# A transformer block on one core: four re-orderings in the first 25 microseconds

## The chip, the cores and the metric

The kernel runs on one core of a Trainium2 chip. A core has five engines that run side by side and wait for one another by semaphores: TensorE (PE, matmuls; PEld is its weight load), VectorE (DVE), ScalarE (ACT), GpSimd (POOL) and SyncE (SP, which here only issues DMAs). Every engine works through its own instructions strictly in the order of the program, so an instruction that waits also holds up all those behind it on its engine. ACT can issue DMAs too. Data lie in SBUF; matmul results go to PSUM, whose banks are handed around.

The metric is the device time of one execution in microseconds; of several runs the median is taken.

## The reference

The kernel computes a layernorm, and from it, in parallel, sliding-window attention and a gated feed-forward network, and adds both to the input:

```
x  = A_x                                   # 1 x 2048 x 448, bf16
xn = (x - mean) / sqrt(var + 1e-5)
q, k, v = xn @ wqkv                        # 16 heads of 28
p  = softmax(q k^T / sqrt(28)), a query sees the 256 keys up to its own
out = x + (p v) @ wo + (gelu(xn @ w_gate) * (xn @ w_up)) @ w_down    # inner width 1792
```

## The kernel before

**Tiling.** The 2048 rows are 16 x tiles of 128 rows, and four query blocks (`qb`) of 512 rows, that is four tiles each. The feature dimension 448 is three chunks of 128 and a half chunk of 64. `xnT` holds the normalised rows transposed, with the half chunk stored twice (partitions 0 to 63 and 64 to 127), so that two half matmuls can run on the two halves of the PE array: `mm3` makes the three full chunks of a product, `mm_half` the half one. A head has 28 columns, but 32 partitions: `wqp`, `wkp` and `w3p` are copies of the q and k weights with heads spread to 32 columns ("padding copies"), made by `pads(engine, dst, groups)`; a group is four heads. `w3p` holds the half chunk of both. Later, `fill_pads` writes into the four spare columns of each head, with nine small copies and then three more and a memset.

**Order.** All instructions are put out in the order written (a manual schedule). The start of the kernel is straight code (lines 662 to 708): for tiles 0 to 3 `stat` (DVE: bn_stats, bn_aggr), `rstd` (ACT: Ln, then Exp of -0.5 times it), `norm` (DVE, and POOL for the last 64 columns of tiles 1 and 2), `transp` (PE transposes, copied from PSUM by ACT or DVE). Between them stand v's products of tiles 0 to 3 (`v_dense` the three chunks, `v_half` the half one, `v_copy` from PSUM to `v_sb`) and the q and k projections of group 0 (`proj`, `qk_halves`, `qk_copies`: q by ACT, k by DVE). `make_masks` (POOL) writes a table needed from query block 1 on.

**The attention of query block 0** has 12 steps, three for each group of four heads. A step: products held back from the step before are finished (`held` feeds: half matmuls and copies), scores (PE, into one PSUM area of four banks that is free again when the Exp of the step before is done), Exp (ACT, L604), masks by `affine_select` (POOL, L518), then filler matmuls from the feeds (projections of the next groups, `gen_up` products, block 1's projections), and at last one entry of `aux`: `ahead` in step 0 (norm of tile 4), `ahead2` in step 1, `ahead3` in step 2, `fill_pads` in steps 3 and 4. The feeds take PSUM banks in the ring m, m, d; a bank can be written again when its earlier content was copied out. In group 1, `gen_qk` gets `others`, the half products of v's tiles 2 and 3 (the "second excursion" to half matmuls); the bank of tile 3's v is the one that group 2's q takes next. Tiles 4 and up are transposed by DMA (`dma_transp`, on SP). After `ahead3`, SP issues the later weights (`loads`).

**Input DMAs** are issued by SP and ACT in the order of lines 126 to 147. Each engine has one queue, and both queues are served by the same 16 DMA engines. L130 (ACT) brings the q and k weights of heads 0 to 3, L138 (SP) those of heads 4 to 15, q's half first, then k's.

After query block 0's attention come, four times, the gated products, and then the attention of the next block mixed with the down projection. The change does not touch these.

Of the kernel before, what the change touches and what calls it, by code (L numbers as in the profile page):

```python
# [15 lines left out]
S, D, H, Dh, F = 2048, 448, 16, 28, 1792  # L16
# [59 lines left out]
def kernel(  # L76
# [11 lines left out]
    nc = tc.nc  # L88
# [18 lines left out]
    xv = A_x.rearrange("b (n p) d -> p (b n) d", p=P)  # L107
# [3 lines left out]
    x_sb = const.tile([P, NT, D], bf16, name="x_sb")  # L111
    wv = const.tile([P, 4, D], bf16, name="wv")
    v_sb = const.tile([P, NT, H, 32], bf16, name="v_sb")
    wraw = blk.tile([P, 4, 2 * D], bf16, name="wraw", tag="hT")
# [7 lines left out]
    def rows(w, c0, n):  # L122
        return w[c0 * P:(c0 + n) * P, :].rearrange("(c p) n -> p c n", p=P)

    wqk = rows(A_wqkv, 0, 3)[:, :, 0:2 * D]
    nc.sync.dma_start(out=x_sb[:, 0, :], in_=xv[:, 0, :])
    nc.scalar.dma_start(out=x_sb[:, 1, :], in_=xv[:, 1, :])
    nc.sync.dma_start(out=x_sb[:, 2:4, :], in_=xv[:, 2:4, :])
    for c in (0, D):
        nc.scalar.dma_start(out=wraw[:, 0:3, c:c + 4 * Dh], in_=wqk[:, :, c:c + 4 * Dh])  # L130
# [38 lines left out]
    wqp = const.tile([P, 3, H, 32], bf16, name="wqp")  # L169
    wkp = const.tile([P, 3, H, 32], bf16, name="wkp")  # L170
    w3p = const.tile([P, H, 32], bf16, name="w3p")
# [15 lines left out]
    def warmup(n):  # L187
        wps = phase[0].pool.tile([P, 2, QB], f32, name="wps", tag="s")
        for i in range(n):
            nc.tensor.matmul(wps[:, i % 2, :], lhsT=warm[:, 0:P], rhs=warm[:, 0:QB], start=True, stop=True)  # L190


    def stat(t):
        st = work.tile([P, nc.vector.BN_STATS_DIM], f32, name="st")
        nc.vector.bn_stats(out=st[:, :], in_=x_sb[:, t, :])  # L195
        nc.vector.bn_aggr(out=mv_all[:, t, :], in_=st[:, :])

    def rstd(t, n):
        lnv = work.tile([P, 4], f32, name="lnv")
        nc.scalar.activation(out=lnv[:, 0:n], in_=mv_all[:, t:t + n, 1], func=ACT.Ln, bias=eps_t[:, 0:1], scale=1.0)  # L200
        nc.scalar.activation(out=rstd_all[:, t:t + n], in_=lnv[:, 0:n], func=ACT.Exp, scale=-0.5)
# [3 lines left out]
    def norm(t):  # L205
        xn = work.tile([P, 4, P], bf16, name="xn", bufs=4)
        xf = xn[:, :, :].rearrange("p a b -> p (a b)")
        for eng, lo, n, src in ((nc.vector, 0, D, 0), (nc.gpsimd if t in (1, 2) else nc.vector, D, 64, 384)):
            eng.tensor_scalar(out=xf[:, lo:lo + n], in0=x_sb[:, t, src:src + n], scalar1=mv_all[:, t, 0:1],
                              scalar2=rstd_all[:, t:t + 1], op0=ALU.subtract, op1=ALU.mult)  # L210
        xns[t] = xn

    def dma_transp(t):

        nc.sync.dma_start_transpose(out=xnT[:, :, t * P:(t + 1) * P], in_=xns.pop(t)[:, :, :].rearrange("p a b -> p (a b)"))

    def transp(t, n, copy, tag):

        tp = psum.tile([P, 2, 4, P], bf16, name="tp", tag=tag, bufs=2 if tag == "m" else 1)
        for i in range(n):  # L220
            xn = xns.pop(t + i)
            for c in range(4):
                nc.tensor.transpose(out=tp[:, i, c, :], in_=xn[:, c, :], identity=ident[:, :])
        copy(out=xnT[:, :, t * P:(t + n) * P].rearrange("p c (i q) -> p i c q", q=P), in_=tp[:, 0:n, :, :])

    def mm3(ps, lhs, rhs, start, stop):
        for c in range(3):
            nc.tensor.matmul(ps, lhsT=lhs(c), rhs=rhs(c), start=start and c == 0, stop=stop and c == 2,  # L228
                             skip_group_check=True)

    def mm_half(ps, lhs, rhs, hi, start, stop):
        p0 = 64 * hi
        nc.tensor.matmul(ps, lhsT=lhs[p0:p0 + 64], rhs=rhs[p0:p0 + 64], start=start, stop=stop,  # L233
                         tile_position=(p0, 0), skip_group_check=True)
# [4 lines left out]
    def bank(name):  # L239

        tag = ring[0][ring[1] % len(ring[0])]
        ring[1] += 1
        return psum.tile([P, QB], f32, name=name, tag=tag, bufs=2 if tag == "m" else 1)


    def v_dense(t, pv):
        mm3(pv, lambda c: xnT[:, c, t * P:(t + 1) * P], lambda c: wv[:, c, :], True, False)

    def v_half(t, pv):
        mm_half(pv, xnT[:, 3, t * P:(t + 1) * P], wv[:, 3, :], t % 2, False, True)  # L250

    def v_copy(t, pv, copy):
        copy(out=v_sb[:, t, :, 0:Dh], in_=pv.rearrange("p (h d) -> p h d", d=Dh))  # L253
# [15 lines left out]
    def proj(ps, w, qb, g):  # L269
        mm3(ps, lambda c: w[:, c, 4 * g:4 * g + 4, :].rearrange("p h d -> p (h d)"), lambda c: xnT[:, c, qb * QB:(qb + 1) * QB],  # L270
            True, False)

    def qk_halves(qb, g, pq, pk):
        w3 = w3p[:, 4 * g:4 * g + 4, :].rearrange("p h d -> p (h d)")
        for hi, ps in enumerate((pq, pk)):
            mm_half(ps, w3, xnT[:, 3, qb * QB:(qb + 1) * QB], hi, False, True)

    def qk_copies(qb, g, pq, pk):
        ts = slice(qb * QB, (qb + 1) * QB)
        nc.scalar.copy(out=qT[:, g, ts], in_=pq)  # L280
        nc.vector.tensor_copy(out=kT[:, g, ts], in_=pk)
        done.add((qb, g))

    def gen_qk(qb, gs, others=()):

        for g in gs:
            pq = bank("pq")[:, :]
            proj(pq, wqp, qb, g)
            if qb and g == 3:
                yield 650  # L290
                ts = slice(qb * QB, (qb + 1) * QB)
                nc.tensor.matmul(pq, lhsT=w3p[:, 12:16, :].rearrange("p h d -> p (h d)"), rhs=xnT[:, 3, ts], start=False, stop=True,
                                 skip_group_check=True)
                nc.scalar.copy(out=qT[:, 3, ts], in_=pq)
                done.add((qb, 3))
                yield -220
                return
            yield 650
            pk = bank("pk")[:, :]
            proj(pk, wkp, qb, g)  # L300
            yield 650, HOLD
            qk_halves(qb, g, pq, pk)
            for t, pv in others:
                v_half(t, pv)
            if others:
                v_copy(*others[1], nc.vector.tensor_copy)
            qk_copies(qb, g, pq, pk)
            others = ()
            yield -360
# [36 lines left out]
    def gen_proj(qb):  # L346
        yield from gen_v(qb, (4 * qb, 4 * qb + 2))
        yield from gen_qk(qb, range(4))
# [299 lines left out]
    def pads(eng, dst, gs):  # L648

        hs = slice(4 * gs.start, 4 * gs.stop)  # L650
        c0 = D * (dst is wkp)
        src = wraw[:, 0:3, c0 + Dh * hs.start:c0 + Dh * hs.stop]
        eng(out=dst[:, :, hs, 0:Dh], in_=src.rearrange("p c (h d) -> p c h d", d=Dh))
# [13 lines left out]
    norm(0)  # L667
    transp(0, 1, nc.scalar.copy, "o")
    stat(2)
    norm(1)  # L670
    rstd(2, 1)
    warmup(1)
    transp(1, 1, nc.scalar.copy, "d")
    stat(3)
# [1 line left out]
    pvs = [bank("pv")[:, 0:D]]  # L676
    v_dense(0, pvs[0])
    norm(2)
    pads(nc.vector.tensor_copy, wqp, slice(0, 1))
    nc.vector.tensor_copy(out=w3p[:, :, 0:Dh], in_=wraw[:, 3, 0:D].rearrange("p (h d) -> p h d", d=Dh))  # L680
    pads(nc.scalar.copy, wkp, slice(0, 1))
    transp(2, 1, nc.scalar.copy, "o")
    pvs.append(bank("pv")[:, 0:D])
    v_dense(1, pvs[1])
    norm(3)
# [4 lines left out]
    pq, pk = (phase[0].pool.tile([P, 2, QB], f32, name="s0", tag="s")[:, 0, :] for _ in range(2))  # L690
    proj(pq, wqp, 0, 0)
    proj(pk, wkp, 0, 0)
    stat(4)
    stat(5)
    rstd(4, 2)
# [1 line left out]
    for t in range(2):  # L697
        v_half(t, pvs[t])
    qk_copies(0, 0, pq, pk)
    for dst in (wqp, wkp):  # L700
        pads(nc.vector.tensor_copy, dst, slice(1, 2))
    v_copy(0, pvs[0], nc.scalar.copy)
    v_copy(1, pvs[1], nc.vector.tensor_copy)
    pvs.append(alone("pv", "d"))
# [9 lines left out]
    def ahead2():  # L714
        stat(6)
        stat(7)
        rstd(6, 2)
        norm(5)
        dma_transp(5)

    def ahead3():
        for t in (6, 7):
            norm(t)
            dma_transp(t)
        v_copy(2, pvs[2], nc.vector.tensor_copy)
        loads()

    def loads():

        nc.sync.dma_start(out=x_sb[:, 12:16, :], in_=xv[:, 12:16, :])  # L730
        nc.sync.dma_start(out=wgu3[0:64, :], in_=B_w_gate[384:448, :])
        nc.sync.dma_start(out=wug3[64:128, :], in_=B_w_gate[384:448, :])
        nc.sync.dma_start(out=wg[:, :, :], in_=rows(B_w_gate, 0, 3))
        wo_v = A_wo.rearrange("(g j d) n -> j d g n", g=4, j=4)
        for j in range(4):
            nc.sync.dma_start(out=wo[32 * j:32 * j + Dh, :, :], in_=wo_v[j])
        for k in range(0, NF, 4):
            n = min(4, NF - k)
            nc.sync.dma_start(out=wd[:, k:k + n, :], in_=rows(B_w_down, k, n))
# [189 lines left out]
```

## Time and profile before

| what | value |
|---|---|
| runs, median of 3 | 223.92 us (223.68 to 224.28) |
| profiled execution: span from first to last instruction | 222.5 us |
| profiled execution: own time | not listed; the median lies 1.42 us above the span |
| PE busy | 211.6 us (95%) |
| DVE busy | 156.3 us (70%) |
| ACT busy | 132.9 us (60%) |
| POOL busy | 44.7 us (20%) |
| mean granted PE clock | 0.994 |
| chain that ended last | PE 91%, DVE 4%, issue 1%, DMA 1% |

How to read it: "busy" is the time in which an engine had an instruction running. The chain that ended last is followed back from the last instruction, at each step to what released it; its shares show where a microsecond counts. Times in rows of the timeline are start and length in us, followed by the engine, the line of the kernel, the operation, what it writes and reads, and in square brackets the idle time before it and what ended it. Rows of one kind that follow each other are merged (x2 is two of them). On DVE and ACT an instruction's row often starts some 0.09 us before the last one's ends. The profiled execution is one, the slowest core's; the runs give the times.

### The profile page before, as it was taken

Reading aid. Unit: us, or ns where it says so; the run is one execution under the profiler, and the core shown is the slowest. Engines: PE = TensorE matmul, PEld = TensorE weight load, DVE = VectorE, ACT = ScalarE, POOL = GpSimd, SP = SyncE. Lnnn points to the kernel's source line nnn. Section 1 sums busy time; section 2 is a strip of 40 time slices with the busy share of each in tenths; the row PEclk is TensorE's granted clock in tenths of the full one; section 3 lists DMA queues with packets and bytes.
Section 4 is the critical chain, followed back from the end, with each engine's and each line's share of the span. In section 5 each row is a group of like instructions: output and inputs, shape, how many; then the busy total and the mean of one; then the engine's idle time right before and its main releaser. Section 6 shows DMA issues by size and latency. Waiting matters only on the chain.

```text
span 222.5 us, 5330 instructions
## 1 busy us (share of the span) xinstructions
PE 211.6 (95%) x2215; PEld 94.5 (42%) x2240; DVE 156.3 (70%) x370; ACT 132.9 (60%) x129; POOL 44.7 (20%) x65
## 2 busy tenths in 40 slices
PE   6899999999999999999999999999999999999990
PEld 2333333344444454444444445444444435434470
DVE  5989996799666983778566895585454999479210
ACT  4597788644878874533868886323767778453000
POOL 5763687320000220022000030022000022022000
PEclk9999999999999999999999999999999999999997
DMA  6994899104100001001500001200000000000011
GB/s 190 312 327 47 195 327 289 20 2 72 45 3 21 24 24 31 16 19 28 70 0 24 24 0 45 43 0 0 0 4 24 24 0 24 21 0 4 22 45 27
DMA packets 18046, 13.31 MB, mean 60 GB/s; under 512 B 8704, under 2 KB 16992, under 8 KB 18016
## 3 DMA queue, kind: packets, MB, share of 16 engines
q1 hardware_dynamic: 17072, 12.62, 21.6%
q8 instruction: 19, 0.31, 0.6%
q10 hardware_dynamic: 944, 0.29, 0.5%
q14 instruction: 11, 0.09, 0.2%
HBM read 9.15 MB, written 2.18 MB: 51 GB/s over the span
## 4 chain that ended last, share of the span: by engine, by line
PE 91%; DVE 4%; issue 1%; DMA 1%; ACT 0%; DVEq 0%
PE po L375 20%; PE gt L228 17%; PE u L228 12%; PE sc L600 6%; PE po L370 6%; PE gt L233 5%; PE ue L228 5%; PE ov L560 5%; PE pq L228 4%; PE pv L228 4%; PE pk L228 3%; PE pq L233 2%; DVE st L195 1%; PE ue L233 1%; DMA x_sb<-in_A_x_dram 1%
## 5 line engine op out<-in xcount | busy, mean ns | idle before, releaser
L604 ACT ACTIVATE p_sb<-sc 128x2048 bf16<-128x2048 f32 (+2 forms) x42 | 73.8, 1758 | 12.6 <-PE sc L600 7.3
L375 PE MATMUL po<-wd,hT 128*128 128x448 bf16 (+1 forms) x238 | 50.0, 342 | 0.0
L452 ACT ACTIVATE ge<-gt 128x1024 bf16<-128x1024 f32 x28 | 28.7, 1024 | 33.6 <-PE u L233 20.9
L527 POOL TENSOR_TENSOR oN<-oc,l 128x512 bf16<-128x512 f32 x12 | 16.0, 1333 | 138.6 <-DVE l L544 88.2
L228 PE MATMUL gt<-xnT,wg 128*128 128x512 bf16 x161 | 38.9, 380 | 1.0 <-issue 0.9
L456 DVE TENSOR_TENSOR hT<-ge,u 128x512 bf16<-128x512 bf16 x40 | 25.6, 682 | 9.7 <-ACT ge L452 9.6
L375 PEld LDWEIGHTS <-hT 128*128 128x128 bf16 x238 | 21.4, 98 | 18.6 <-issue 2.6
L228 PE MATMUL u<-xnT,wu 128*128 128x512 bf16 x116 | 28.8, 379 | 0.2
L508 DVE TENSOR_TENSOR p_sb<-p_sb,masks 128x256 bf16<-128x256 bf16 (+1 forms) x90 | 27.2, 356 | 0.4 <-ACT p_sb L604 0.4
L228 PEld LDWEIGHTS <-wg 128*128 128x128 bf16 x168 | 15.1, 98 | 21.5 <-issue 5.2
L228 PEld LDWEIGHTS <-wu 128*128 128x128 bf16 x168 | 16.0, 98 | 19.2 <-issue 1.0
L549 DVE TENSOR_TENSOR oc<-oc,ov 128x512 f32<-128x512 f32 x12 | 8.3, 688 | 18.3 <-ACT oc L548 18.3
L600 PE MATMUL sc<-qT,kT 28*64 28x320 bf16 (+7 forms) x640 | 16.9, 263 | 0.1
L380 DVE TENSOR_TENSOR res<-po,x_sb 128x448 bf16<-128x448 f32 (+1 forms) x17 | 9.9, 585 | 8.7 <-PE po L375 8.6
L370 PE MATMUL po<-wo,oN 128*128 128x448 bf16 (+1 forms) x68 | 15.9, 343 | 0.0
L518 POOL TENSOR_SCALAR_AFFINE_SELECT p_sb<-p_sb 128x512 bf16<-128x512 bf16 (+1 forms) x20 | 14.2, 731 | 8.3 <-ACT p_sb L604 8.1
L409 DVE CAST hT<-ue 128x512 bf16<-128x512 f32 x16 | 10.2, 680 | 6.3 <-PE ue L233 6.2
L548 ACT COPY oc<-ov 128x512 f32<-128x512 f32 x12 | 7.0, 584 | 11.9 <-PE ov L560 11.9
L233 PE MATMUL gt<-xnT,wgu 64*128 64x512 bf16 x48 | 13.2, 379 | 0.0
L228 PE MATMUL pq<-xnT,wqp 128*128 128x512 bf16 x36 | 11.7, 380 | 0.7 <-DVE v_sb L253 0.3
L534 DVE STREAM_TRANSPOSE l<-oc 128x512 f32<-128x512 f32 x16 | 11.3, 704 | 1.4 <-POOL oN L527 1.2
L228 PE MATMUL ue<-xnT,wu 128*128 128x512 bf16 x43 | 11.6, 380 | 0.4 <-issue 0.2
(87 smaller groups left out, 235.4 us busy)
## 6 DMA issues: line engine op xcount, KB each, us to landing
out_dram<-res SPq DMA_DIRECT2D x15, 112.0 KB
x_sb<-in_A_x_dram SPq DMA_DIRECT2D x3, 448.0 KB
wu<-in_B_w_up_dram SPq DMA_DIRECT2D x1, 1344.0 KB
wg<-in_B_w_gate_dram SPq DMA_DIRECT2D x1, 1344.0 KB
wd<-in_B_w_down_dram SPq DMA_DIRECT2D x3, 448.0 KB
wraw<-in_A_wqkv_dram SPq DMA_DIRECT2D x2, 252.0 KB
wo<-in_A_wo_dram SPq DMA_DIRECT2D x4, 98.0 KB
wv<-in_A_wqkv_dram SPq DMA_DIRECT2D x1, 336.0 KB
```

Of the source, the lines that this page charges most:

```text
L228: nc.tensor.matmul(ps, lhsT=lhs(c), rhs=rhs(c), start=start and c == 0, stop=stop and c == 2, skip_group_check=True)
L233: nc.tensor.matmul(ps, lhsT=lhs[p0:p0 + 64], rhs=rhs[p0:p0 + 64], start=start, stop=stop, tile_position=(p0, 0), skip_group_check=True)
L370: nc.tensor.matmul(po[:, 0:w], lhsT=oN[:, g, cs], rhs=wo[:, g, lo:up], start=(g == 0), stop=False, skip_group_check=True)
L375: nc.tensor.matmul(po[:, 0:w], lhsT=hT[:, f, cs], rhs=wd[:, f, lo:up], start=False, stop=(f == NF - 1), skip_group_check=True)
L452: nc.scalar.activation(out=ge[:, :, :], in_=pr["gt"][:, :, :], func=ACT.Gelu_apprx_tanh)
L456: nc.vector.tensor_tensor(out=hT[:, f + i, :], in0=ge[:, i, :], in1=u[:, :], op=ALU.mult)
L508: nc.vector.tensor_tensor(out=reg, in0=reg, in1=m, op=ALU.mult)
L518: nc.gpsimd.affine_select(out=reg, in_=reg, pattern=mid + [[1 if diag else -1, min(w, P)]], compare_op=ALU.is_ge, fill=0.0, base=0 if diag ...
L527: nc.gpsimd.tensor_tensor(out=oN[:, g, :], in0=oc[:, :], in1=inv, op=ALU.mult)
L534: nc.vector.transpose(out=l1[:, :, :].rearrange("p a b -> p (a b)"), in_=oc[:, :])
L600: nc.tensor.matmul(ss[k0:k0 + nk, j, col:col + nq], lhsT=kT[r, g, kt * P + k0:kt * P + k0 + nk], rhs=qT[r, g, qb * QB + q0:qb * QB + q0 + ...
L604: nc.scalar.activation(out=p_sb[:, :, 0:ncol], in_=ss[:, :, 0:ncol], func=ACT.Exp, scale=SCALE)
```

## The change

The diff has five places.

1. Tile 0 of x is loaded in two halves of 64 partitions, one by SP and one by ACT. Tile 1 moves from ACT's queue to SP's, ahead of tiles 2 and 3.
2. The first padding copies (group 0): `wqp` goes from DVE to ACT, `wkp` stays on ACT, and both now stand behind `transp(2)`'s copy; `w3p`'s copy goes from DVE to POOL, behind the norms of tiles 1 and 2 and ahead of `make_masks`.
3. The second ones (group 1) go from DVE, where they stood behind group 0's k copy, to ACT, ahead of `rstd(4, 2)`.
4. In `gen_qk`, v's half products stand ahead of `qk_halves` where there are any (group 1 of block 0).
5. `rstd(6, 2)` (Ln and Exp on ACT) moves from `ahead2` (step 1) to the head of `ahead3` (step 2).

`rstd(2, 1)` is also written ahead of `norm(1)`; the two have no engine in common, so each engine's order stays the same.

```diff
-    nc.sync.dma_start(out=x_sb[:, 0, :], in_=xv[:, 0, :])
-    nc.scalar.dma_start(out=x_sb[:, 1, :], in_=xv[:, 1, :])
+    nc.sync.dma_start(out=x_sb[0:64, 0, :], in_=xv[0:64, 0, :])
+    nc.scalar.dma_start(out=x_sb[64:128, 0, :], in_=xv[64:128, 0, :])
+    nc.sync.dma_start(out=x_sb[:, 1, :], in_=xv[:, 1, :])
...
             yield 650, HOLD
-            qk_halves(qb, g, pq, pk)
             for t, pv in others:
                 v_half(t, pv)
+            qk_halves(qb, g, pq, pk)
...
     stat(2)
+    rstd(2, 1)
     norm(1)
-    rstd(2, 1)
...
     norm(2)
-    pads(nc.vector.tensor_copy, wqp, slice(0, 1))
-    nc.vector.tensor_copy(out=w3p[:, :, 0:Dh], in_=wraw[:, 3, 0:D].rearrange("p (h d) -> p h d", d=Dh))
-    pads(nc.scalar.copy, wkp, slice(0, 1))
     transp(2, 1, nc.scalar.copy, "o")
+    for dst in (wqp, wkp):
+        pads(nc.scalar.copy, dst, slice(0, 1))
+    nc.gpsimd.tensor_copy(out=w3p[:, :, 0:Dh], in_=wraw[:, 3, 0:D].rearrange("p (h d) -> p h d", d=Dh))
...
     proj(pk, wkp, 0, 0)
+    for dst in (wqp, wkp):
+        pads(nc.scalar.copy, dst, slice(1, 2))
     stat(4)
     stat(5)
     rstd(4, 2)
...
     qk_copies(0, 0, pq, pk)
-    for dst in (wqp, wkp):
-        pads(nc.vector.tensor_copy, dst, slice(1, 2))
     v_copy(0, pvs[0], nc.scalar.copy)
...
     def ahead2():
         stat(6)
         stat(7)
-        rstd(6, 2)
         norm(5)
         dma_transp(5)
...
     def ahead3():
+        rstd(6, 2)
         for t in (6, 7):
```

## The prediction

> **What bounds the kernel now.** I read four views in this order: busy time by stretch, the chain of waits in order of time, who waited for whom, and the timeline of single engines. The table by stretch comes first (columns: busy us and count of PE, PE weight loads, DVE, ACT, POOL, then clock, DMA share, GB/s).
>
> ```profile
> 14.70:20.00 5.30, 4.58 (x33) 1.69 (x34) 5.20 (x13) 4.16 (x8) 3.46 (x5) 1.00 0.56 133
> 20.00:26.00 6.00, 5.95 (x47) 2.18 (x47) 5.89 (x22) 4.52 (x4) 3.36 (x6) 1.00 0.74 103
> 26.00:36.40 10.40, 10.29 (x97) 4.00 (x98) 10.06 (x23) 9.39 (x10) 7.77 (x10) 1.00 1.07 318
> ```
>
> From 18.5 us on PE has no idle time to speak of, so a microsecond that it is early or late there is kept to the end. But DVE is just as full from 14.7 to 36.4 us: PE can only stay ahead by what DVE gains too. Everything the change touches ends before 26 us.
>
> ```profile
> 7.45 0.89 DVE wqp L653
> 8.34 0.12 DVE w3p L680
> 8.46 0.31 DVE xn L209
> ...
> 14.73 0.62 DVE v_sb L253
> ...
> 17.46 0.30 ACT lnv L200
> 17.79 0.20 ACT rstd_all L201
> 17.99 0.48 ACT qT L280
> ```
>
> These are the pieces of the chain that the edits aim at: the padding copies between two norms, v's copy, and the Ln/Exp that holds up a q copy.
>
> **The first x tile.** DVE's first statistics wait 1.25 us for x and start at 3.40, when tile 0 has landed. Tiles 0 and 1 share the DMA engines (between 2.4 and 2.8 us the two queues carry 53% and 48%); at that window's 327 GB/s, 224 KB take 0.7 us, so tile 0 alone lands up to 0.35 us earlier. I take 0.3 (0 to 0.4). Tile 1 now follows on SP at 1.26 us; with tile 0's 2.58 us from issue to landing it is there at 3.84, when the second statistics would start (4.17 - 0.33). No cost. But every later load of SP moves back by one issue of about 0.45 us (0.40 to 0.48 in the rows).
>
> **The first padding copies.** They leave DVE's order between norm(2) and norm(3), where wqp and w3p take 7.45 to 8.46.
>
> ```profile
> 7.42 0.85 POOL L155 MEMSET masks<- 128x768 bf16 x1
> 7.45 0.89 DVE L653 COPY wqp<-wraw 128x336 bf16<-128x336 bf16 x1
> 7.91 0.46 ACT L653 COPY wkp<-wraw 128x336 bf16<-128x336 bf16 x1
> 11.23 0.29 ACT L200 ACTIVATE lnv<-mv_all,eps_t 128x2 f32<-128x2 f32 x1 [2.38 <-DVE mv_all L196]
> ```
>
> The reader should see that DVE's copy takes 0.89 us here and 0.28 at 12.22: it ends 0.07 after the POOL memset at its side. This pattern returns below. norm(3) would be bound by its own Exp instead: 8.00 less 0.3, so 7.7 in place of 8.38. On POOL the w3p copy costs between 0.63 (a 512-column select) and 1.27 us (L527, two inputs); I take 0.8, from about 7.3, with the memset of masks behind it. norm(3) is a copy-like DVE op from SBUF to SBUF and can be held in the same way: its start lies between 7.7 and, behind both POOL ops, 9.4. I take 8.1, a gain of 0.3; the masks have until the Exp of step 0 (14.75) and end near 14.1. ACT's two copies (2 x 0.46 behind transp(2)'s copy at 8.0 to 8.6) end near 9.1, before PE needs wqp and wkp near 9.5 and 10.1.
>
> **The second copies, ahead of rstd(4).** ACT idles 2.38 us before 11.23, and two copies of 0.46 look free. But wkp's heads 4 to 7 come with the last of L138's loads. Up to it queue q1 carries 1.89 MB (sizes of the DMA list); it had moved 1.92 MB by 9.5 us, some of it already wu's, and the trace's completion records of that load end at 10.55, two engines late. The extra SP issue moves that to 10.7 to 11.0; I take L = 10.85. Queued behind the waiting copy on ACT: Ln 0.29 and Exp 0.20 of rstd(4), qT's copy 0.57, v_sb's copy 0.54. With the overlaps of the rows (each starts some 0.09 before the last ends) qT ends at L + 1.39 and v_sb at L + 1.83, and PE's next projection, which reuses v_sb's bank, starts at 12.71. It starts at 12.72 now. So the gain of some 0.6 us at the start is taken back by this wait: net 0 (0.3 gained if L is 10.55; 0.3 lost if it is 11.1 or norm(3) is held long). DVE loses two copies of 0.28 and 0.25 at 12.22, where it has slack until 14.73: nothing.
>
> **v's half tiles first.** Their matmuls start at 14.11 instead of 14.33, so DVE's v_sb copy and PE's pq behind it (it waits 0.26 for that copy) come 0.22 earlier; q's copy on ACT starts 14.73 instead of 14.64, hidden behind Exp 0, which ends at 14.75.
>
> **Ln/Exp a step later.**
>
> ```profile
> 15.19 1.45 ACT L604 ACTIVATE p_sb<-sc 128x1536 bf16<-128x1536 f32 x1
> 17.46 0.29 ACT L200 ACTIVATE lnv<-mv_all,eps_t 128x2 f32<-128x2 f32 x1 [0.82 <-DVE mv_all L196]
> 18.36 1.03 ACT L604 ACTIVATE p_sb<-sc 128x1024 bf16<-128x1024 f32 x1
> 19.68 0.58 ACT L280 CAST qT<-pq 128x512 bf16<-128x512 f32 x1 [0.29 <-PE pk L233]
> ```
>
> Without the 0.82 us of waiting, qT of group 2 starts at 16.97 (its matmuls end at 17.18 - 0.23), the Exp of step 2 runs 17.45 to 18.48 instead of 18.36 to 19.39, and PE's 0.36 us wait at pk goes. Behind it now stand Ln and Exp (0.42, to 18.90), then qT of group 3 (18.89, before 19.68) and the Exp of step 3, which ends at 21.26 instead of 22.04. norm(6) waits for that Exp until 18.92 and for POOL's select of step 2 (18.54 to 19.2), before 18.79. The four norms, v_copy(2) and kT follow: kT ends near 21.13, before 21.33. SP's transposes of tiles 6 and 7 and the loads behind them move by under 0.2 us; PE reads those tiles at 26.4 and wg at 39.5. So ACT and PE gain 0.78 here, DVE only 0.20.
>
> **What is late next.** DVE's nine small copies of fill_pads come right after kT.
>
> ```profile
> 20.66 0.67 DVE L281 CAST kT<-pk 128x512 bf16<-128x512 f32 x1
> 21.26 0.15 DVE L318 COPY wqp<-wraw 128x16 bf16<-128x16 bf16 x1
> ...
> 21.90 0.16 DVE L320 COPY wkp<-wraw 128x48 bf16<-128x48 bf16 x1
> 21.98 1.27 DVE L409 CAST hT<-ue 128x512 bf16<-128x512 f32 x2
> ...
> 22.11 1.68 POOL L518 TENSOR_SCALAR_AFFINE_SELECT p_sb<-p_sb 128x1024 bf16<-128x1024 bf16 x2 [1.94 <-ACT p_sb L604]
> ```
>
> They end at 22.06 and POOL's selects of step 3 start at 22.11: they just miss. Afterwards the copies run 21.06 to 21.86 and the selects start at 21.33, whatever the start of the kernel gains, since both hang on the Exp of step 2. DVE ops from SBUF to SBUF that meet a POOL op end just after it: norm(5) took 0.72 instead of 0.37 beside the select that ended at 17.93, the last norm 0.60 instead of 0.29 beside 19.46 to 20.18. No row shows small copies in that place. Their price is 0 if they slip through, 1.1 (the 128x1024 select) if they are held once, 1.7 if also by the second. A row decides for held once: 48 columns take only 10 ns longer than 16 (164 against 155), which is the fast rate of the copies that were held (116 to 130 ns for 336 columns more), not that of a cast from PSUM (680 ns for 512).
>
> [...]
>
> **Sum.** Held once, hT's copies start at 22.9 instead of 21.98, then 0.68 + 0.68 + the oc copy 0.68 + fill_pads' second part 0.5; hT of the next pair is copied by 25.80 instead of 25.02. PE's matmul pv, which started right at that copy (25.08), starts at 25.83: +0.75, with 0 from the start of the kernel. Span 222.5 + 0.75 = 223.25. The profiled execution's own time is not listed; the median 223.92 of the runs lies 1.42 above its span, and I keep that: 224.67, rounded 224.7.
>
> **Rivals.**
> 1. Held by both selects (norm(5), issued at 17.34 just as one select followed another, waited for the second): 0.6 more, 225.3.
> 2. The small copies slip through, the other side. Then PE gains only DVE's part: hT's copy at 24.80 in place of 25.02 (PE can't use its 0.76 us, its bank is freed then), -0.26: 223.65. The edits would do what they say locally and little at the end.
> 3. As 2, and the second wraw load is not later than now (L at most 10.5): another 0.4, 223.25 or less. It decides below an L of about 10.5; for it: only two of the sixteen completions came after 9.95. Against it: SP issues it all behind one more load.
> 4. L that early, but the copies are held: 224.3.
>
> **Chances.** Forecast 0.40, its own range 224.3 to 225.1; rival 1 0.20; rival 2 0.16; rival 3 0.16; rival 4 0.08. 0.3% is 0.67 us (also about what a measurement here can tell from no change): faster is below 223.25, slower above 224.59. Faster: most of rival 3 and some of 2, 0.17. Slower: all of rival 1 and three quarters of the forecast, 0.50. Same: 0.33. The range 223.1 to 225.5 takes in all cases but the ends of 1 and 3.
>
> **What would show it.** The first statistics near 3.1; norm(3) near 8.1; ACT idle until 10.7 to 11.0 before the second wkp copy and qT at 11.7; PE's pq of group 1 still near 12.7; no wait of pk on qT; the Exp of step 3 over near 21.3; the nine copies torn apart, one or more above 0.5 us beside a POOL select. If these keep 0.16 us, or if the start is 0.3 us ahead at 12.7, the forecast is wrong.

## The result, and the profile after

| | before | after |
|---|---|---|
| runs, median | 223.96 us (223.68 to 224.28, 6 runs) | 227.26 us (226.75 to 228.94, 6 runs) |
| profiled execution: span | 222.5 us | 225.2 us (own time 226.97) |
| mean granted PE clock | 0.994 (profiled execution) | 0.997 (profiled execution; 0.992 to 0.999 in the runs) |
| last residual (DVE `res`) starts | 217.34 | 219.65 |

The kernel became slower: the ratio is 1.0147, with a 95% interval of 1.0128 to 1.0167. The prediction was 224.7, with a range of 223.1 to 225.5.

The busy time by stretch, for the same three stretches as before (columns as there):

```profile
14.70:20.00 5.30, 5.14 (x35) 1.81 (x37) 4.03 (x9) 4.87 (x7) 3.26 (x5) 1.00 0.96 178
20.00:26.00 6.00, 4.67 (x46) 1.65 (x44) 5.86 (x18) 3.85 (x4) 3.26 (x5) 1.00 0.45 74
26.00:36.40 10.40, 10.08 (x84) 3.72 (x82) 9.99 (x26) 8.28 (x9) 6.19 (x8) 1.00 1.05 292
```

In the second stretch PE is busy for 4.67 us in place of 5.95, while DVE is as full as before (5.86). In the first, PE is busier than before (5.14 against 4.58), though the work in it is not quite the same, since the kernel is some 1.1 us late there: the two waits that the change aimed at, PE's 0.26 us for v's copy and 0.36 us for qT behind Ln/Exp, are gone. The loss lies on both sides of it. The chain of waits in order of time (start, length, what) names both places:

```profile
12.53 0.53 DVE v_sb L254
13.06 0.31 DVE wqp L654
...
13.39 0.40 PE sc L601 x8
...
13.83 0.81 PE pq L229 x3
...
21.79 0.60 DVE kT L282
...
22.63 1.00 DVE wqp L319
...
23.79 0.43 DVE wqp L319
...
24.38 1.19 DVE hT L410 x2
```

The first place is group 1's projection, `pq` at 13.83, which stood at 12.72 before. The timeline of ACT shows why:

```profile
9.74 0.47 ACT L654 COPY wqp<-wraw 128x336 bf16<-128x336 bf16 x1 [0.23 <-DMA wraw<-in_A_wqkv_dram]
11.97 0.47 ACT L654 COPY wkp<-wraw 128x336 bf16<-128x336 bf16 x1 [1.75 <-DMA wraw<-in_A_wqkv_dram]
...
12.78 0.57 ACT L281 CAST qT<-s 128x512 bf16<-128x512 f32 x1
13.24 0.54 ACT L254 CAST v_sb<-pv 128x448 bf16<-128x448 f32 x1
```

The second wkp copy waits 1.75 us for the last load of q and k weights, which lands at 11.94 (10.55 before). Ln, Exp, qT's copy and v's copy stand behind it on ACT. The scores need qT, which is there at 13.35, and start at 13.39; `pq` comes behind the scores and behind v's copy, which ends at 13.78. (The chain puts the scores' wait down to DVE's `wqp` copy, which runs beside them; the scores read qT and kT.)

The second place is the nine small copies. Here are DVE, POOL and PE in their timelines (one fence for each):

```profile
22.31 0.16 DVE L319 COPY wqp<-wraw 128x16 bf16<-128x16 bf16 x1
...
22.55 1.08 DVE L319 COPY wqp<-wraw 128x16 bf16<-128x16 bf16 x1
23.54 0.17 DVE L321 COPY wqp<-wraw 128x48 bf16<-128x48 bf16 x1
23.63 0.16 DVE L321 COPY wkp<-wraw 128x48 bf16<-128x48 bf16 x1
23.72 0.50 DVE L319 COPY wqp<-wraw 128x16 bf16<-128x16 bf16 x1
...
24.30 1.27 DVE L410 CAST hT<-ue 128x512 bf16<-128x512 f32 x2
```

```profile
22.49 1.71 POOL L519 TENSOR_SCALAR_AFFINE_SELECT p_sb<-p_sb 128x1024 bf16<-128x1024 bf16 x2 [2.16 <-ACT p_sb L605]
```

```profile
25.03 0.81 PE L229 MATMUL ue<-xnT,wu 128*128 128x512 bf16 x3 [1.33 <-DVE hT L410]
```

Two of the nine take 1.08 and 0.50 us in place of 0.16, each ending just behind a select. hT's copies start at 24.30 (21.98 before), and PE waits 1.33 us for them. Counted by the starts of the Exp instructions, the kernel is 1.03 us late in step 0, 1.12 in step 1, 0.23 in step 2, 0.38 in steps 3 and 4, 1.87 in step 5 and 2.30 in step 6, and stays 2.30 late to the last residual. Another 0.4 us lies between the start of the last residual and the end of the span (5.6 against 5.2 us). That stretch took 5.2 to 5.9 us in the seven profiles of kernels that split tile 0, and 4.7 to 5.4 us in the nine of kernels that do not. Whether the split causes this was not tested, and what makes the stretch vary was not looked for.

### The profile page after: what moved, and what is told of

It is laid out like the page before. It is cut to its first block, busy times and chain, and to the rows that moved or that the text cites. A ratio compares the mean times of both kernels' runs of the same rounds, so it can differ in the third digit from the quotient of the medians.

```text
span 225.2 us, 5357 instructions
## 1 busy us (share of the span) xinstructions
PE 214.1 (95%) x2240; PEld 94.8 (42%) x2240; DVE 156.6 (70%) x366; ACT 134.3 (60%) x132; POOL 44.9 (20%) x66
## 3 DMA queue, kind: packets, MB, share of 16 engines
HBM read 9.15 MB, written 2.18 MB: 50 GB/s over the span
## 4 chain that ended last, share of the span: by engine, by line
PE 89%; DVE 6%; ACT 1%; DMA 1%; issue 0%; DVEq 0%
PE po L376 20%; PE gt L229 17%; PE u L229 12%; PE po L371 6%; PE sc L601 6%; PE gt L234 5%; PE ov L561 4%; PE pq L229 4%; PE ue L229 4%; PE pv L229 3%; PE pk L229 3%; PE pq L234 1%; DMA x_sb<-in_A_x_dram 1%; DVE xn L210 1%; PE pv L234 1%; PE ue L234 1%
## 5 line engine op out<-in xcount | busy, mean ns | idle before, releaser
L229 PE MATMUL gt<-xnT,wg 128*128 128x512 bf16 x168 | 40.3, 380 | 0.0
L229 PE MATMUL ue<-xnT,wu 128*128 128x512 bf16 x48 | 12.2, 380 | 1.3 <-DVE hT L410 1.3
L254 DVE CAST v_sb<-pv 128x448 bf16<-128x448 f32 x13 | 7.7, 614 | 7.0 <-PE pv L234 7.0
L229 PE MATMUL pq<-xnT,wqp 128*128 128x512 bf16 x45 | 12.2, 380 | 0.2
```

## The experiments

The loss has two candidates, so the runs undo single parts in the changed kernel (first four), make single parts alone in the kernel before (the next), and then take the two costs by themselves. "Before" in each is the kernel before on the same chip: 224.2 us beside the first four, 224.09 beside the next three and the variant with parts 2, 4 and 5, 224.31 beside the order, split and three-warm-up kernels and part 5 with the copies out of the way, 224.28 beside the five warm-ups and the last kernel. A kernel is compared by how far its median lies above that of its own before; for the whole change that is 3.30 us. Behind it stands the ratio with its 95% interval, which is the better guide where the runs spread: part 1 alone lies 1.41 us above by medians and 1.8 by its ratio.

### Undoing one part of the change

**Second padding copies back on DVE** (part 3 undone):

```diff
-    for dst in (wqp, wkp):
-        pads(nc.scalar.copy, dst, slice(1, 2))
...
     qk_copies(0, 0, pq, pk)
+    for dst in (wqp, wkp):
+        pads(nc.vector.tensor_copy, dst, slice(1, 2))
```

> The change with its third part undone: group 1's padding copies are back on DVE, behind k's copy of group 0. Theory (two losses that add: ACT waits about 1.1 us for the second q/k weight load at L139, and fill_pads' small copies are held 1.2 to 1.4 us by POOL's selects): the start is back, PE's projection of group 1 starts at 12.4 to 12.8 instead of 13.83, the small copies are still torn apart; 225.2 us (224.8 to 225.8). Rival (the lost time is the DMA order's, through whatever waits for loads): the start stays late, above 226.3. Rival (one loss only, the wait on ACT): 224.0 or less.

Measured: 226.52 us (226.07 to 227.33), 1.0097 (1.0077 to 1.0116). It lies 2.32 above before, so part 3, with its wait on ACT, costs about 1.0 in the changed kernel, but most of the loss stays: the time is above the range expected, where the rival (the DMA order) had it. The small copies are held in it as in the changed kernel (1.09 and 0.51 us). Its profiled execution was the slowest of its four runs and showed something else: v's first products take 581 ns each, in place of 352, until about 10.8 us; three of them take 1.33 us in place of 0.73, so one starts every 0.38 us in place of 0.19, and "half speed" stands for that here. This is taken up below.

**Ln/Exp back in step 1** (part 5 undone):

```diff
         stat(7)
+        rstd(6, 2)
         norm(5)
...
     def ahead3():
-        rstd(6, 2)
```

> The change with its fifth part undone: Ln/Exp of tiles 6 and 7 are back in step 1. Theory: the Exp of step 3 comes later against DVE's copies again, none of fill_pads' nine copies takes above 0.3 us; the 1.1 us at the start stay, less the 0.2 us of v's half tiles first: 225.0 us (224.6 to 225.6). Rival (moving Ln/Exp is a gain by itself, the loss is all at the start): slower than the whole change, 227.5.

Measured: 225.95 us (224.73 to 226.63, 7 runs), 1.0076 (1.0049 to 1.0103), 1.75 above before, 1.55 less than the whole change. The nine copies run from 21.83 to 22.64, none above 0.17 us, and the selects start at 22.73: as in the kernel before, they just miss. So the collision is the work of part 5. What is left, with a wide spread between runs, is not, and it is more than the theory had (225.6 at most).

**Tiles 0 and 1 of x as before** (part 1 undone):

```diff
-    nc.sync.dma_start(out=x_sb[0:64, 0, :], in_=xv[0:64, 0, :])
-    nc.scalar.dma_start(out=x_sb[64:128, 0, :], in_=xv[64:128, 0, :])
-    nc.sync.dma_start(out=x_sb[:, 1, :], in_=xv[:, 1, :])
+    nc.sync.dma_start(out=x_sb[:, 0, :], in_=xv[:, 0, :])
+    nc.scalar.dma_start(out=x_sb[:, 1, :], in_=xv[:, 1, :])
```

> The change with its first part undone: x tiles 0 and 1 are loaded as before, by SP and ACT. Theory: one SP issue less ahead of L139's loads brings the second of them back to 10.6 to 10.9 us (11.94 in the change), so the wkp copy on ACT waits about 1 us less; first statistics at 3.4 instead of 3.57; fill_pads still held: 225.8 us (225.2 to 226.4). Rival (the load is late because of single DMA engines that lag, not because of the order): 227.0 to 227.3, with the load still landing after 11.5.

Measured: 225.84 us (225.68 to 226.06), 1.0071 (1.0054 to 1.0087), 1.64 above before, 1.66 less than the whole change, and the spread of the runs shrinks from 2.2 to 0.4 us. The last load of q and k weights lands at 10.71:

```profile
10.73 0.47 ACT L653 COPY wkp<-wraw 128x336 bf16<-128x336 bf16 x1 [0.48 <-DMA wraw<-in_A_wqkv_dram]
```

The Exp of step 1 is 0.38 us late here, that of step 2 is 0.51 ahead, and the two held copies (1.08 and 0.51) turn 0.37 ahead into 1.57 behind. This is the prediction's picture, without the late loads.

**Memsets in place of the nine copies.**

```diff
-                put(wqp[:, c, :, :], k, 4, 0)
-                put(wkp[:, c, :, :], k, 3, 4)
+                for dst, n in ((wqp, 4), (wkp, 3)):
+                    if n == 4:
+                        nc.vector.memset(dst[:, c, 12:16, Dh:32], 0.0)
+                    nc.vector.memset(dst[:, c, 0:12, Dh:32], 0.0)
```

> The change with the nine small copies of fill_pads' first part replaced by nine memsets of zero on the same places (this leaves out the packing of group 3's spare columns for blocks 1 to 3, the same number of instructions stays). Memsets on DVE beside POOL ops were not stretched in the trace of before. Theory (the copies are held by POOL's selects): all nine take under 0.2 us, hT's copies start near 22.95 instead of 24.30, and the time falls by 1.2 to 1.4 us to 226.0 (225.6 to 226.4). Rival (DVE is late because norm(6) waits for ACT's Exp, the selects are only beside it): a fall of 0.3 us or less.

Measured: 226.22 us (225.77 to 226.94), 1.0092 (1.0064 to 1.0121). No memset takes more than 0.08 us, and the stretch adds 0.16 us after step 4 where the copies added 1.92:

```profile
23.21 0.08 DVE L328 MEMSET wqp<- 128x24 uint32 x1
23.24 0.66 DVE L411 CAST hT<-ue 128x512 bf16<-128x512 f32 x1
23.25 0.08 DVE L328 MEMSET wkp<- 128x24 uint32 x1
```

The selects of this kernel run from 23.18 on, so only the last three of the nine memsets start behind one, by 0.07 us at most. Nine memsets also take less time than nine copies that are not held: from the start of kT's copy to that of hT's it is 0.84 us here, 1.32 in the kernel before and 2.59 in the changed one. So of the 1.76 saved some 0.5 is the shorter instruction, and the rest, 1.27, the hold. The kernel lies 2.02 above before, 1.28 less than the whole change. In the profiled execution PE was at half speed until about 11 us and the Exp of step 0 came 1.81 late.

### One part alone in the kernel before

**Part 1 alone:**

```diff
-    nc.sync.dma_start(out=x_sb[:, 0, :], in_=xv[:, 0, :])
-    nc.scalar.dma_start(out=x_sb[:, 1, :], in_=xv[:, 1, :])
+    nc.sync.dma_start(out=x_sb[0:64, 0, :], in_=xv[0:64, 0, :])
+    nc.scalar.dma_start(out=x_sb[64:128, 0, :], in_=xv[64:128, 0, :])
+    nc.sync.dma_start(out=x_sb[:, 1, :], in_=xv[:, 1, :])
```

> Part 1 alone on the kernel before. Theory A (the split of tile 0 makes everything behind it later: issues of 64 rows take 0.59 us in place of 0.40, tiles 2 and 3 and v's weights land later, PE idles ahead of tile 1's transposes and some executions then run their first matmuls at half speed until about 11 us): first statistics no earlier than 3.4, third statistics (tile 2) after 5.8, Exp of step 0 at 13.1 to 14.6 in place of 12.87, time 0.3 to 1.7 us above before, with a spread of over 1 us between runs. Theory B (the split is harmless; what it cost in the full change it cost only because the padding copies on ScalarE waited for the last wraw load, and here DVE's do not reach that point before it has landed): within 0.3 us of before, with before's spread. The prediction's step (tile 0 lands 0.3 us earlier) would give 0 to 0.3 us less.

Measured: 225.5 us (225.31 to 226.67), 1.0080 (1.0057 to 1.0103). Theory A: the split costs on its own, by some 1.4 us, and spreads the runs. The first statistics start at 3.50 (3.40 before), not earlier, and the third at 5.71 (5.38), a little earlier than theory A had. The profile is of the fastest run (225.31), and in it the body of the kernel is only 0.35 late; another 0.73 us is lost behind the start of the last residual. So this profile shows only a part of the price at the start of the kernel. The timelines of SP show where it begins, before first, then the changed kernel:

```profile
0.80 0.40 SPq L126 DMA_DIRECT2D x_sb<-in_A_x_dram  x1
1.26 0.43 SPq L128 DMA_DIRECT2D x_sb<-in_A_x_dram  x1
```

```profile
0.81 0.59 SPq L126 DMA_DIRECT2D x_sb<-in_A_x_dram  x1
1.45 0.56 SPq L128 DMA_DIRECT2D x_sb<-in_A_x_dram  x1
2.06 0.43 SPq L129 DMA_DIRECT2D x_sb<-in_A_x_dram  x1
```

Issuing half a tile takes 0.59 us, longer than the whole tile's 0.40, and tile 1's issue 0.56 (0.82 in the profile of part 1 alone). So tiles 2 and 3 (the row at 1.26 before, at 2.06 after) are issued 0.80 us later, or 1.06. The DMA view between 1 and 5 us shows what is lost, before first, then the changed kernel:

```profile
DMA packets 1462, 0.87 MB, mean 218 GB/s; under 512 B 625, under 2 KB 1462, under 8 KB 1462
```

```profile
DMA packets 1341, 0.67 MB, mean 168 GB/s; under 512 B 758, under 2 KB 1341, under 8 KB 1341
```

0.20 MB less has moved. At the 320 GB/s or so of the busy stretches (318 in the kernel before between 26.0 and 36.4 us) that is 0.6 us for all that follows, by estimate. By 10.5 us 0.37 MB are missing (2.18 against 2.55), some 1.2 us at that rate, and so late is the last load of q and k weights; why the gap grows between 5 and 10.5 us was not looked for. That load's own issue is no later (over at 7.18 us, 7.38 before): what came late is the bytes ahead of it in the queue.

**Part 5 alone:**

```diff
         stat(7)
-        rstd(6, 2)
...
     def ahead3():
+        rstd(6, 2)
```

> Part 5 alone on the kernel before. Theory A (the gain on ScalarE turns into a collision): Exp of step 3 some 0.8 us earlier, the nine small copies begin near 21.1 and POOL's selects near 21.3, one copy is held for 1.0 to 1.1 us and another for about 0.5, hT's copies start 0.7 to 1.7 us later than at 21.98; time 0.6 to 1.6 us above before. Theory B (the collision needs the whole change): no copy above 0.2 us, hT's copies at about 21.8, time 0.2 us below before to equal.

Measured: 225.79 us (225.46 to 226.01), 1.0072 (1.0058 to 1.0086). Theory A:

```profile
21.77 1.09 DVE L318 COPY wqp<-wraw 128x16 bf16<-128x16 bf16 x1
...
22.94 0.51 DVE L318 COPY wqp<-wraw 128x16 bf16<-128x16 bf16 x1
...
23.53 0.68 DVE L409 CAST hT<-ue 128x512 bf16<-128x512 f32 x1
```

The Exp of step 4 is 0.40 us ahead of the kernel before, that of step 6 is 1.52 behind it, and so is the last residual. A wait taken from ACT alone makes the kernel 1.7 us slower.

**Parts 2, 3 and 4 together**, without 1 and 5 (part 4's lines stand for the three):

```diff
-            qk_halves(qb, g, pq, pk)
             for t, pv in others:
                 v_half(t, pv)
+            qk_halves(qb, g, pq, pk)
```

> Parts 2, 3 and 4 without the split of tile 0 and without the later Ln and Exp. Theory A (the loss comes from parts 1 and 5): the second wkp copy waits on ScalarE for its load until about 10.7, PE's projection of group 1 starts near 13.0 (12.72 before), no small copy above 0.2 us; 0 to 0.4 us above before. Theory B (the padding copies on ScalarE ahead of rstd(4) are a cause of their own): 0.7 us or more above before.

Measured: 224.36 us (223.81 to 225.04, 11 runs), 1.0009 (0.9996 to 1.0021). Theory A: no measurable difference. The load lands near 10.77, group 1's pq starts at 12.97. Part 4's gain can be read between two steps: the Exp of step 1 is 0.27 late, that of step 2 only 0.04, so 0.23 us, where 0.22 was forecast.

The medians add up: 1.41 (part 1), 1.70 (part 5) and 0.27 (parts 2 to 4) are 3.38 us; the whole change cost 3.30. The close match is in part luck: parts 1 and 5 alone make 3.11, but the changed kernel without part 3 lies only 2.32 above before. Part 3 costs little by itself and about 1.0 behind a late load, and the intervals are some 0.3 to 0.6 us wide to each side.

### What the split of tile 0 costs, and how

**The order without the split.**

```diff
     nc.sync.dma_start(out=x_sb[:, 0, :], in_=xv[:, 0, :])
-    nc.scalar.dma_start(out=x_sb[:, 1, :], in_=xv[:, 1, :])
+    nc.sync.dma_start(out=x_sb[:, 1, :], in_=xv[:, 1, :])
```

> The kernel before with tile 0 whole on SP and tile 1 behind it on SP too: the extra issue on SP without the split. Theory A1 (the 64-row issue is what makes the later loads late): tiles 2 and 3 are issued some 0.4 us later than before, in place of 0.6; time 0 to 0.4 us above before. Theory A2 (the extra load on SP's queue does it): third statistics after 5.8, time 0.7 to 1.5 us above before, as with part 1 alone.

Measured: 225.71 us (224.43 to 226.82, 8 runs), 1.0064 (1.0036 to 1.0092). **The split without the order:**

```diff
-    nc.sync.dma_start(out=x_sb[:, 0, :], in_=xv[:, 0, :])
+    nc.sync.dma_start(out=x_sb[0:64, 0, :], in_=xv[0:64, 0, :])
+    nc.scalar.dma_start(out=x_sb[64:128, 0, :], in_=xv[64:128, 0, :])
     nc.scalar.dma_start(out=x_sb[:, 1, :], in_=xv[:, 1, :])
```

> The kernel before with tile 0 split between SP and ScalarE, and tile 1 left on ScalarE: the split without the extra issue on SP. Theory A1 (the 64-row issue is what makes the later loads late): tiles 2 and 3 about 0.2 us later than before, tile 1 and ScalarE's q and k weights 0.6 later, time 0.3 to 1.2 us above before. Theory A2 (the extra load on SP's queue does it): within 0.3 us of before.

Measured: 226.55 us (225.52 to 226.62, 5 runs), 1.0079 (1.0057 to 1.0101). Neither theory holds alone: the extra load on SP costs without the 64-row issue, and the 64-row issue costs without the extra load, by more than either theory had. In both profiles the third statistics, those of tile 2, start late, at 5.95 and 6.01: with the order alone they wait 0.58 us for tile 2, with the split alone the second ones wait 0.69 us for tile 1. In the profile of the order PE is at full speed, and the Exp of step 0 is 0.82 late, so late loads have a price of their own. In that of the split it is 1.62 late, and PE at half speed until about 11 us. The runs of these kernels fall in clusters (the split alone: three near 226.6 and two at 225.5), for which late loads alone give no reason.

**More warm-up matmuls with part 1.**

```diff
-    warmup(1)
+    warmup(3)
     transp(1, 1, nc.scalar.copy, "d")
```

> Part 1 alone on the kernel before, with three warm-up matmuls in place of one ahead of tile 1's transposes, so that PE's idle time there (0.6 to 1.0 us) is filled. Theory A (part of the price of late tiles is PE at half speed until about 11 us, because it idles there): v's first products take 352 ns each in every execution, no run is over 1 us above the lowest, median 0.3 to 1.0 us below that of part 1 alone (1.4 us above before). Theory B (the price is the late loads alone): 1.2 to 1.8 us above before, as with part 1 alone.

Measured: 225.27 us (225.13 to 226.0), 1.0048 (1.0032 to 1.0064): 0.96 above before where part 1 alone was 1.41 above. v's first products take 353 ns, as theory A has it, but the intervals of the two kernels overlap and the runs still spread by 0.9 us. That does not settle it.

**Fewer warm-up matmuls in the kernel before**, so that PE idles and no load is touched:

```diff
-    warmup(8)
+    warmup(5)
     stat(0)
```

> The kernel before with five warm-up matmuls in place of eight at the start, so that PE idles about 1.3 us more ahead of tile 0's transposes; no load is touched. Theory A (an idle PE at the start is what leaves it at half speed): v's first products take 581 ns each in place of 352, until 9 us or later, the Exp of step 0 comes 0.4 to 1.6 us later than 12.87 with tiles 2 and 3 landing as before, time 0.4 to 1.6 us above before in all or many runs. Theory B (half speed comes from something else, and only late loads cost): 352 ns from v's first product on, time within 0.3 us of before.

Measured: 225.44 us (224.96 to 225.76), 1.0057 (1.0040 to 1.0074). Theory A. The timelines of PE, before first:

```profile
6.79 0.73 PE L228 MATMUL pv<-wv,xnT 128*128 128x448 bf16 x3
...
7.82 0.73 PE L228 MATMUL pv<-wv,xnT 128*128 128x448 bf16 x3
```

```profile
5.26 0.61 PE L223 MATMUL tp<-ident,xn 128*128 128x128 bf16 x4 [0.98 <-DVE xn L209]
...
6.90 1.33 PE L228 MATMUL pv<-wv,xnT 128*128 128x448 bf16 x3
...
8.45 1.33 PE L228 MATMUL pv<-wv,xnT 128*128 128x448 bf16 x3
```

Three products take 1.33 us in place of 0.73, up to 11 us, while tile 2 is there as before (third statistics at 5.32). The Exp of step 0 is 1.51 late, and so is the rest. An idle PE in the first microseconds has a price of its own, here 1.16 us of the median. In the kernels with part 1, some executions pay it and some do not: the changed kernel's profile does not (352 ns from 6.96 on, yet its last warm-up at half speed, of 634 ns, starts at 4.92, where the kernel before is at full speed from 4.88, with 379 ns), those of part 3 undone, of the memsets and of the split alone do. In these three PE idles 0.40 to 0.72 us before it has reached full speed, because tile 1 or tile 2 of x is late. In the profile of the order alone it kept full speed, once reached, through a longer gap (1.26 us), and in that of the kernel before through one of 0.58 us. How often it happens in the changed kernel was not counted, so how much of part 1's price is half speed stays open.

### Can the gain of part 5 be had?

**Part 5 alone, with the copies out of the way.** The nine copies go behind norm(7), where POOL has no select, and v's copy goes ahead of the norms, where DVE waits for the Exp of rstd(6):

```diff
     def ahead3():
+        rstd(6, 2)
+        v_copy(2, pvs[2], nc.vector.tensor_copy)
         for t in (6, 7):
             norm(t)
             dma_transp(t)
-        v_copy(2, pvs[2], nc.vector.tensor_copy)
+        fill_pads(False)
         loads()
...
-                aux = [ahead, ahead2, ahead3, lambda: fill_pads(False), lambda: fill_pads(True), lambda: None,
+                aux = [ahead, ahead2, ahead3, lambda: None, lambda: fill_pads(True), lambda: None,
```

> Part 5 alone on the kernel before, with the nine small copies moved behind norm(7) into ahead3, and v_copy(2) moved to the head of the norms, where DVE would otherwise wait for the Exp of rstd(6). Theory A (part 5's gain is real once DVE neither waits for it nor meets a select): v_copy(2) runs near 18.8, norm(6) near 19.4, the nine copies from about 20.5 to 21.3 at 0.16 us each, hT's copies start 0.2 to 0.5 us ahead of 21.98; time 0.2 to 0.5 us below before. Theory B (DVE has no room in this stretch, whatever the order): hT's copies at 21.9 or later, time equal to before within 0.3 us.

Measured: 224.2 us (223.69 to 224.48, 11 runs), 0.9995 (0.9986 to 1.0004): equal to before. No copy is above 0.16 us, the Exp of step 4 is 0.33 early, hT's copies start at 21.82, and the last residual of that profile is 0.19 early. A variant with parts 2, 4 and 5, in which v's copy stayed behind the norms and the nine copies went ahead of it, shows why the place of v's copy matters:

```diff
             dma_transp(t)
+        fill_pads(False)
         v_copy(2, pvs[2], nc.vector.tensor_copy)
```

> Parts 2, 4 and 5 on before's loads, and the nine small copies of fill_pads stand ahead of v_copy(2) in ahead3, where POOL has no select to run. Theory A (part 5 is a gain if the copies miss the selects): copies run from about 20.0 to 20.9 at 0.16 us each, hT's copies start 0.2 to 0.6 us ahead of 21.98, time 0.2 to 0.6 us below before. Theory B (v_sb's and kT's copies, now 0.8 us behind the nine, hold PE's banks): PE waits for kT or v_sb between 20 and 23, time equal to before or up to 0.5 us above.

Measured: 224.42 us (223.79 to 224.72, 11 runs), 1.0014 (1.0004 to 1.0025). The nine copies miss the selects (20.25 to 21.06), but norm(6) waits for its Exp, kT's copy comes at 21.51 and hT's at 22.11: 0.69 us ahead in step 2 are down to nothing in step 4. Theory B.

**Parts 4 and 5 with the first of these orders**, which adds to it:

```diff
-            qk_halves(qb, g, pq, pk)
             for t, pv in others:
                 v_half(t, pv)
+            qk_halves(qb, g, pq, pk)
```

> Parts 4 and 5 on the kernel before, with the nine small copies behind norm(7) and v_copy(2) at the head of the norms (the kernel with part 5 alone and this order came to the Exp of step 4 0.32 us early, the end 0.19 early). Theory A (part 4's 0.23 us adds, since it lies upstream of ScalarE and DVE alike): Exp of step 4 0.4 to 0.6 us early, hT's copies near 21.6, time 0.3 to 0.5 us below before. Theory B (DVE sets hT's copies, and what PE and ScalarE gain is lost there): hT's copies at 21.8 again, time equal to before within 0.25 us.

Measured: 223.81 us (223.36 to 223.97, 12 runs) against 224.28, 0.9981 (0.9972 to 0.9990). Theory A: 0.2% below before, a small gain clear of the noise. From DVE's timeline:

```profile
18.70 0.61 DVE L253 CAST v_sb<-pv 128x448 bf16<-128x448 f32 x1
19.23 1.11 DVE L209 TENSOR_SCALAR xn<-x_sb,mv_all,rstd_all 128x448 bf16<-128x448 bf16 x4
...
20.90 0.17 DVE L320 COPY wkp<-wraw 128x48 bf16<-128x48 bf16 x1
20.98 0.68 DVE L281 CAST kT<-pk 128x512 bf16<-128x512 f32 x1
21.58 1.28 DVE L409 CAST hT<-ue 128x512 bf16<-128x512 f32 x2
```

v's copy fills the wait, norm(6) starts at 19.23, and the copies are over before the selects start at 21.54. The Exp of step 4 is 0.57 us early, the last residual 0.43. Neither the new order nor part 4 was run by itself, so it is not shown how the gain is shared between them and part 5.

## Why the prediction was wrong, step by step

**The first x tile: this step failed.** It said that tile 0 lands 0.3 us earlier and that the later loads of SP move back by one issue of about 0.45 us, at no cost. The first statistics started 0.17 later (3.57), not 0.3 earlier; in the seven profiles with the split they start at 3.23 to 3.60, against 3.40 before. The bytes were halved, but the issue of a half takes 0.59 us, and no row of the trace of before had a 64-row issue of x; the 64-row issues of weights behind it in SP's row (0.57 to 0.59) were the nearest rows and were not used. Tiles 2 and 3 were issued 0.80 later in place of 0.45. "No cost" was the term that failed: part 1 alone costs 1.41 us, by late loads and, in some executions, by late tiles that leave PE idle and so at half speed (581 ns in place of 352), which was not thought of.

**The second copies: the mechanism was right, its L was not.** qT was to end at L + 1.39, v's copy at L + 1.83, with pq right behind. With the measured L of 11.94 that is 13.33, 13.77 and some 13.8; measured were 13.35, 13.78 and 13.83. But L was taken as 10.85 (10.7 to 11.0). Without part 1 it is 10.71 to 10.77, so the rest of the step stands: part 1 moved it by 1.2 us in this execution (0.95 in that of part 5 undone, 11.66). The forecast let one more issue of SP move the landing by 0.15 to 0.45 us; the bytes that had not moved early on (0.37 MB by 10.5 us) moved it by more. The net 0 at 12.72 became 1.11.

**The first padding copies** came out near the forecast: norm(3) starts at 8.20 (8.1). The w3p copy on POOL took 0.56 us, below the lower bound of 0.63. norm(3) itself takes 0.78 us (0.38 before) beside POOL's memset of masks (8.11 to 8.84), so nothing of the earlier start arrives at PE.

**v's half tiles first and Ln/Exp later** were right: the kernel wins back 0.89 us between steps 1 and 2, the forecast's 0.82 of waiting and 0.22 of part 4 overlapping in 0.91 (18.36 to 17.45). That DVE gains little was right too; it gained 0.06 (kT 1.05 late where the start was 1.11 late) and not 0.20, since norm(6) waited 0.42 for the Exp of rstd(6).

**What is late next** was right, and mis-sized. The copies are held by both selects: one copy takes 0.92 us longer behind the first, another 0.34 behind the second. The nine and the hand-over to hT's copies take 1.99 us in place of 0.72, so 1.27 for being held, between the forecast's 1.1 and rival 1's 1.7. By what a select holds a copy, no run shows.

The forecast took the nine copies for alike; the rows show a difference. All eight copies that are held, in the profiles of the change, of parts 1 and 3 undone and of part 5 alone, have 16 columns. In each of the four, a 16-column copy that starts 0.06 or 0.07 us behind the first select is held to that select's end, and a 48-column copy that starts 0.07 us behind the second (which starts at 23.56 in the changed kernel) takes its usual 0.16 us. So the forecast's reading of the 48-column copies, that their rate is that of copies that can be held, finds no support in these rows. Whether their form spares them, or the moment between two selects, no run here tells.

**The sum** had a slip: hT's copies 0.92 late (22.9 against 21.98) should have stayed 0.92 late at the next pair, as the spacing of the two pairs did not change (2.35 us before, 2.34 after); the text let 0.17 of it go. In all, the forecast's 0.75 and 1.11 from L, 0.14 from DVE, 0.17 from the held copies (1.27 against 1.1) and 0.17 from the sum make 2.34; the body of the kernel shows 2.30. The median moved by more than that: 0.4 at the end of the span, and 0.3 twice, since the profiled execution of before lies that far above its median (a run with that span of 222.5 took 224.26) and that of after (226.97) below its own.

**Rivals.** The third, an early L, was the opposite of what happened; no rival had an L above the stated bound. The second, copies that slip through, is what part 5 undone shows, for another reason: there nothing moved them. Slower at one in two was the right side, and for the held copies the right reason; the 1.11 us at the start, a third of the loss, were not behind it.

## What to carry to other kernels

Price a split of a DMA by its issues too, not by its bytes alone, and follow the queue behind it to the first engine that waits for its last load: here a load meant to start the kernel 0.3 us earlier moved one that lands 8 us after it by 1.2. When an instruction is moved onto an engine ahead of others, write its end as "landing plus so much"; the sum is then as good as the bound on the landing, and a wide bound belongs in the range. A wait taken away from a tight order moves all that follows it against the other engines: look for the pair that now meets (here small copies and selects, which missed each other by 0.05 us), and move that pair apart in the same edit.

## What the runs showed of the hardware

- An issue of 64 rows of x took 0.57 to 0.59 us (the changed kernel and part 1 alone), one of 128 rows 0.40 (the kernel before); tile 1's whole issue behind the half one took 0.56 us in the changed kernel and 0.82 with part 1 alone.
- In the four profiles in which PE idled for 0.40 to 0.98 us in the first microseconds, before it had reached full speed (five warm-up matmuls, part 3 undone, the memsets, the split alone), it stayed at half speed to about 11 us (products of 581 ns in place of 352); in the kernel with five warm-up matmuls that was worth 1.16 us of the median. Once at full speed it kept it through gaps of 0.58 us (the kernel before) and 1.26 us (the order alone). The granted clock in the views does not tell the two apart: it shows 1.00 between 2 and 5 us of the kernel before, where most warm-up matmuls take 634 ns and the last 379; the durations of the matmuls tell. The first matmuls at full speed start at 4.88 in the kernel before, by 5.78 in the changed kernel, by 6.90 with part 1 alone, and at about 11 where PE idled. What sets that moment, no run shows.
- In four profiles (the change, parts 1 and 3 undone, part 5 alone) a DVE copy of 16 columns that started 0.06 or 0.07 us behind a POOL select took 1.08 or 1.09 us in place of 0.16. No copy of 48 columns was held, even 0.07 us behind a select's start, and no memset: one that starts 0.17 us behind a select in the last kernel takes 0.11 us, and so does one that starts 0.02 us behind a select in the kernel before (24.16 and 24.14).
